# Retention attention and two feed-forward layers on one core: the causal upper quarter left out of the score products of eleven chunks, and the last output tile drained in two halves

## The chip, the cores and the metric

One core of a Trainium2 chip runs the kernel. The metric is the device time of one execution in microseconds, the median over runs of the same kernel. A profile of one execution goes with it: every instruction of every engine with its start and its length.

## What is computed

Four sequences of 576 tokens, eight heads of 64, pass through a causal attention without softmax whose scores are damped by a power of the distance, and then through two feed-forward layers. All of it is float32.

```python
scores = scale * np.matmul(q, k.transpose(0, 1, 3, 2))
Dmat = np.where(rel >= 0, gamma[:, None, None] ** rel[None, :, :], 0.0)   # rel = query - key position
ret = np.matmul(scores * Dmat, v)                     # x: (2304, 512) after the heads are joined
h = x @ w_in;  g = np.maximum(h, 0) + alpha * np.minimum(h, 0);  x = g @ w_out        # d_ff 2048
gate = 1 / (1 + np.exp(-(x @ w_gate)));  out = (gate * (x @ w_val)) @ w_out2          # d_ff 1536
```

## The kernel before, in words

The 2304 tokens are cut into five blocks (one of 256 tokens, four of 512) and, for the attention, into 20 chunks that lie inside one block and one sequence. Sixteen chunks have 128 tokens, four have 64. A chunk is processed as a step of a recurrence. The scores of the chunk's queries with the chunk's keys are formed (`att_scores`), multiplied by a 0/1 triangle on VectorE (the "mask"), and multiplied with the values (`att_values`). What earlier chunks of the sequence give is carried in a state `m_sb` (64x64 for each head): the queries are multiplied with it, and it is updated by the product of the chunk's keys and values. The damping sits in per-row factors that GpSimd multiplies into the queries (`att_q`, tile `qk`) and the values (`att_v`, tile `kv`) of the next chunk ahead of time.

Chunks 0 to 6 (blocks 0 and 1) run first, on banks of their own. Chunks 7 to 10 (block 2), 11 to 15 (block 3) and 16 to 19 (block 4) run in `att_stages`, in two stages each that are placed between the steps of the first feed-forward layer: a step `h` (12 products of 512 columns) and a step `y` (12 more). TensorE's order is the order of the code. For a chunk of 128 tokens in these blocks it reads: 8 score products (L571), a step of the layer, 8 products for the state's update (`m`, L597, absent for the last chunk of a sequence), 8 products of the queries with the old state (L600, absent for the first chunk of a sequence), 8 products of the scores with the values (L611), the next step. Chunk 10 begins a sequence; chunks 9 and 19 end one. Chunks 14 and 15 have 64 tokens.

All attention products are float32, and each is carried out as two passes, so that 8 products are 16 instructions in the trace. The products of the layers use split factors, with one instruction each (L700). A product with 64 rows or 64 columns of the array uses a part of it: the score products use 64 rows and 128 columns (written 64\*128 in the trace), the updates and the values 128\*64, the old state 64\*64. Two or four such products, on different parts, can be under way at once. The results of L600 and L611 add up in two banks, `o_0` and `o_1`, that held the scores `s_0` and `s_1`; so L600 waits until the masks of the chunk (L574, two on VectorE) have read them.

The order of the other engines' instructions is set by a scheduler at build time, with the times of a model. Each engine works off its instructions in that order, GpSimd too, and waits with all that is behind it when the first one waits. SyncE issues all transfers from one queue. At the end of the program, the last of 24 steps of the second layer's last block adds into two output tiles; ScalarE copies the first to SBUF, VectorE the second (`drain`, L733 to L740), and SyncE stores each.

Of the kernel before, what the change touches and what calls it, by code (L numbers as in the profile page):

```python
# [19 lines left out]
P = 128  # L20
# [66 lines left out]


CHUNKS = chunks()
LENGTHS = sorted({c[3] for c in CHUNKS})  # L90


O_M = NPAIR * P
O_GK = O_M + P
O_GP = O_GK + H
O_M2 = O_GP + len(LENGTHS) * NPAIR
O_GK2 = O_M2 + D
N_CST = O_GK2 + NPAIR


def constants():
    gamma = (1.0 - 2.0 ** (-5.0 - np.arange(H, dtype=np.float32))).astype(np.float64)
    i = np.arange(P)
    head = 2 * np.arange(NPAIR)[None, :] + (i // D)[:, None]
    out = np.zeros((P, N_CST), np.float32)
    out[:, :O_M] = (gamma[head][:, :, None] ** i / np.sqrt(D)).reshape(P, -1)
    out[:, O_M:O_GK] = i[None, :] >= i[:, None]
    out[:, O_GK:O_GP] = gamma ** -i[:, None].astype(np.float64)
    out[:, O_GP:O_M2] = (gamma[head][:, None, :] ** np.array(LENGTHS)[None, :, None]).reshape(P, -1)

    out[:, O_M2:O_GK2] = i[None, :D] >= i[:, None] % D
    out[:, O_GK2:] = gamma[head] ** -(i[:, None] % D).astype(np.float64)
    return out

# [2 lines left out]
def retention_two_ffn(ctx: ExitStack, tc: tile.TileContext, att, cst, alpha, w1, w2, out0, out1):  # L117
# [44 lines left out]
    mask = c_sb[:, O_M:O_GK]  # L162
    decay = c_sb[:, :O_M].rearrange("p (a i) -> p a i", a=NPAIR)


# [363 lines left out]
    def att_v(n):  # L529

        v = raw_a[n][1][:, 1]
        heads = v.shape[1]
        gk = O_GK if heads == H else O_GK2
# [10 lines left out]
    def att_scores(n, pool, tags):  # L544

        c = CHUNKS[n][3]
        qk = raw_a[n][0]
        if c < P:
            if len(tags) == 1:
                ps = pool.tile([P, 2, DM], F32, tag=tags, name=f"s{n}")[:, 0, :NPAIR * c]  # L550
                ps = ps.rearrange("p (a i) -> p a i", a=NPAIR)
            else:
                ps = pool.tile([P, NPAIR, c], F32, tag=tags[0], name=f"s{n}")
            for pr, e in HEADS:
                nc.tensor.matmul(ps[part(e), pr, :], qk[part(e), 1, pr, :], qk[part(e), 0, pr, :], start=True, stop=True)
            by = c_sb[:, O_M2:O_GK2].unsqueeze(1).to_broadcast([P, NPAIR, c])
            nc.vector.tensor_tensor(out=qk[:, 1], in0=ps, in1=by, op=ALU.mult)
            return qk[part(0), 1], qk[part(1), 1]
        if len(tags) == 1:
            ps = pool.tile([P, 2, DM], F32, tag=tags, name=f"s{n}")  # L560
            for pr, e in HEADS:
                nc.tensor.matmul(ps[:, e, pr * P:(pr + 1) * P], qk[part(e), 1, pr, :], qk[part(e), 0, pr, :], start=True, stop=True)
            s_sb = both_scores[n] = slot([P, 2, NPAIR, P], F32, f"sc{n}")
            nc.vector.tensor_tensor(
                out=s_sb.rearrange("p e a i -> p (e a) i"), in0=ps.rearrange("p e (a i) -> p (e a) i", a=NPAIR),
                in1=mask.unsqueeze(1).to_broadcast([P, H, c]), op=ALU.mult,
            )
            return s_sb[:, 0], s_sb[:, 1]
        ps = [pool.tile([P, NPAIR, P], F32, tag=tags[e], name=f"s{n}_{e}") for e in range(2)]
        for pr, e in HEADS:  # L570
            nc.tensor.matmul(ps[e][:, pr, :], qk[part(e), 1, pr, :], qk[part(e), 0, pr, :], start=True, stop=True)  # L571
        s_sb = qk[:, 1], small.tile([P, NPAIR, P], F32, tag="s", bufs=3, name=f"sc{n}")
        for e in (1, 0):
            nc.vector.tensor_tensor(  # L574
                out=s_sb[e], in0=ps[e], in1=mask.unsqueeze(1).to_broadcast([P, NPAIR, c]), op=ALU.mult,
            )
        return s_sb

    def att_values(n, s_sb, pool, tags):
# [13 lines left out]
        rows = lambda t, pr, e: kv[part(e), t, pr] if c < P else kv[:, t, 2 * pr + e]  # L593
        if not last:
# [3 lines left out]
        if pos:  # L598
            for pr, e in HEADS:
                nc.tensor.matmul(  # L600
                    out(pr, e), m_sb[part(e), pr, :], qk[part(e), 0, pr, :], start=pr < 2, stop=False,
                )
# [7 lines left out]
        for pr, e in HEADS:  # L610
            nc.tensor.matmul(  # L611
                out(pr, e), rows(1, pr, e), s_sb[e][:, pr, :], start=pos == 0 and pr < 2, stop=pr >= 2,
            )
# [563 lines left out]
    def plain_y(ps, g, f, first, last):  # L1177
        w = plain_outer[f]
        for e, t in enumerate(ps):

            r = tuple(w[:, :, i] for i in range(2))
            products(t.rearrange("p (c j) -> p c j", c=2), [(cols(g, e), r)], first, last)
            if last:
                drain(e, f"ost0_{e}", t, out0[e * P:(e + 1) * P, :])

    def plain_z(f, ws):
        nb = BLOCKS[0]
# [309 lines left out]
```

## Time and profile before

| | |
|---|---|
| median of 3 runs | 863.33 us (863.12 to 864.38) |
| the profiled execution's own time | 862.71 us |
| its span in the profile | 860.9 us |
| TensorE | 844.4 us busy, 98% |
| VectorE | 547.9 us, 64% |
| ScalarE | 419.7 us, 49% |
| GpSimd | 97.3 us, 11% |
| granted TensorE clock | 1.0 throughout |

A line of the timeline has the start in us, the length in us, the engine, the source line, the operation, the tiles (output<-inputs, without their numbers), the part of the array (rows\*columns) and the operand sizes, the count of instructions that are merged in it, and in brackets the idle time before it with what ended that. Matmul instructions overlap, so the time that a group of products costs is read from its start to the start of the next group, not from the length. In a line that ends in us, times, longest, the three figures are total waiting, count and the longest wait. PE is TensorE, DVE is VectorE, ACT is ScalarE, POOL is GpSimd, SP is SyncE.

### The profile page before, as it was taken

Reading aid. Unit: us, or ns where it says so; the run is one execution under the profiler, and the core shown is the slowest. Engines: PE = TensorE matmul, PEld = TensorE weight load, DVE = VectorE, ACT = ScalarE, POOL = GpSimd, SP = SyncE. Lnnn points to the kernel's source line nnn. Section 1 sums busy time; section 2 is a strip of 40 time slices with the busy share of each in tenths; the row PEclk is TensorE's granted clock in tenths of the full one; section 3 lists DMA queues with packets and bytes.
Section 4 is the critical chain, followed back from the end, with each engine's and each line's share of the span. In section 5 each row is a group of like instructions: output and inputs, shape, how many; then the busy total and the mean of one; then the engine's idle time right before and its main releaser. Section 6 shows DMA issues by size and latency. Waiting matters only on the chain.

```text
span 860.9 us, 13167 instructions
## 1 busy us (share of the span) xinstructions
PE 844.4 (98%) x4898; PEld 704.9 (82%) x4898; DVE 547.9 (64%) x840; ACT 419.7 (49%) x724; POOL 97.3 (11%) x72
## 2 busy tenths in 40 slices
PE   6899999999999999999999999999999999999998
PEld 5798888777778887888888888888888888888897
DVE  4899863785786969997647675469813332695111
ACT  1777754453564769986336653345412222352111
POOL 5357623223100000000000000000000000000000
PEclk9999999999999999999999999999999999999999
DMA  9658999699977125899967999255896561569970
GB/s 341 228 186 274 348 402 365 221 358 407 417 263 280 49 91 194 294 364 346 409 222 274 411 417 407 103 196 192 294 394 228 187 199 69 172 223 371 366 285 26
DMA packets 81728, 234.04 MB, mean 272 GB/s; under 512 B 8576, under 2 KB 9600, under 8 KB 81664
## 3 DMA queue, kind: packets, MB, share of 16 engines
q1 hardware_dynamic: 81664, 233.20, 73.9%
q8 instruction: 39, 0.64, 0.3%
q14 instruction: 25, 0.20, 0.1%
HBM read 169.72 MB, written 63.44 MB: 271 GB/s over the span
## 4 chain that ended last, share of the span: by engine, by line
PE 78%; DVE 1%; DMA 1%; ACT 1%; issue 0%; SPq 0%; DVEq 0%; ACTq 0%
PE a L700 15%; PE yy L700 10%; PE oa L700 8%; PE y L700 6%; PE h L700 5%; PE a_h L700 5%; PE z L700 4%; PE c L700 4%; PE b L700 4%; PE e L700 4%; PE o L700 2%; PE oc L700 2%; PE ob L700 2%; PE oe L700 2%; PE b_h L700 1%; PE c_h L700 1%
## 5 line engine op out<-in xcount | busy, mean ns | idle before, releaser
L700 PE MATMUL h<-x,w 128*128 128x512 f32 (+1 forms) x432 | 84.1, 346 | 2.1 <-DVE t L720 1.3
L700 PEld LDWEIGHTS h<-x,w 128*128 128x128 f32 x432 | 67.5, 190 | 12.6 <-DVE t L720 1.9
L700 PE MATMUL y<-g,w 128*128 128x512 f32 x240 | 58.9, 394 | 0.0
L336 ACT ACTIVATE q<-r 128x512 fp32r<-128x512 f32 x72 | 45.2, 664 | 24.3 <-PE yy L700 9.1
L231 POOL TENSOR_SCALAR r<-r 128x512 int32<-128x512 uint32 x26 | 51.9, 1996 | 42.2 <-DMA r<-w 30.1
L337 DVE TENSOR_TENSOR q<-r,q 128x512 fp32r<-128x512 f32 x72 | 49.3, 709 | 9.7 <-ACT q L336 9.7
L716 ACT ACTIVATE t<-h 128x512 f32<-128x512 f32 (+1 forms) x48 | 25.0, 521 | 57.8 <-PE h L700 57.8
L700 PEld LDWEIGHTS y<-g,w 128*128 128x128 f32 x240 | 44.4, 188 | 10.2 <-issue 1.0
L1029 DVE TENSOR_TENSOR c<-a,es 128x512 f32<-128x512 f32 x24 | 16.7, 699 | 55.3 <-PE a L700 55.3
L229 ACT ACTIVATE r<-r 128x512 f32<-128x512 f32 x68 | 45.0, 669 | 8.2 <-DMA r<-w 6.3
L238 DVE CUSTOM_DVE_ANT_0 r<-r,top 128x1024 uint16<-128x1024 uint16 x52 | 35.6, 696 | 2.3 <-POOL r L231 0.5
L700 PEld LDWEIGHTS z<-x,zp 128*128 128x128 f32 x288 | 36.0, 191 | 0.9
L700 PE MATMUL z<-x,zp 128*128 128x256 f32 x288 | 36.3, 283 | 0.0
L700 PE MATMUL h<-x,v 128*128 128x512 f32 x144 | 35.4, 395 | 0.0
L700 PE MATMUL y<-g,v 128*128 128x512 f32 x144 | 35.2, 393 | 0.0
L700 PEld LDWEIGHTS y<-g,v 128*128 128x128 f32 x144 | 26.7, 188 | 6.1 <-issue 0.7
L700 PE MATMUL a<-xf_1h,tq 128*128 128x512 f32 x96 | 31.5, 389 | 0.0
L700 PE MATMUL e<-xf_5h,tq 128*128 128x512 f32 x96 | 31.5, 389 | 0.0
L700 PE MATMUL a<-xf_6h,tq 128*128 128x512 f32 x96 | 31.5, 389 | 0.0
L700 PE MATMUL b<-xf_2h,tq 128*128 128x512 f32 x96 | 31.5, 389 | 0.0
L700 PE MATMUL a<-xf_7h,tq 128*128 128x512 f32 x96 | 31.5, 389 | 0.0
L700 PE MATMUL c<-xf_3h,tq 128*128 128x512 f32 x96 | 31.5, 389 | 0.0
(468 smaller groups left out, 2130.9 us busy)
## 6 DMA issues: line engine op xcount, KB each, us to landing
tq<-td SPq DMA_DIRECT2D x84, 512.0 KB, 7.1
r<-w SPq DMA_DIRECT2D x68, 512.0 KB, 6.5
wo<-wod SPq DMA_DIRECT2D x42, 512.0 KB, 4.8
v<-w1d SPq DMA_DIRECT2D x40, 512.0 KB, 6.0
td<-q SPq DMA_DIRECT2D x36, 512.0 KB, 5.1
wod<-q SPq DMA_DIRECT2D x24, 512.0 KB, 8.7
zp<-td SPq DMA_DIRECT2D x48, 256.0 KB, 5.8
w1d<-w SPq DMA_DIRECT2D x23, 512.0 KB, 8.5
```

Of the source, the lines that this page charges most:

```text
L229: nc.scalar.activation(high.bitcast(F32), high.bitcast(F32), AF.Prelu, scale=2.0 ** -112, alpha=2.0 ** 32)
L231: nc.gpsimd.tensor_scalar(low.bitcast(I32), low, 2.0 ** -29, None, ALU.mult)
L238: nc.vector.tensor_tensor(out=out.bitcast(I32), in0=low.bitcast(I32), in1=top.bitcast(I32), op=ALU.add)
L336: nc.scalar.activation(part[0], src, AF.Copy)
L337: nc.vector.tensor_tensor(out=part[1], in0=src, in1=part[0].bitcast(F32), op=ALU.subtract)
L700: nc.tensor.matmul(ps, l, r, start=first and i == 0, stop=last and i == len(todo) - 1, skip_group_check=joins)
L716: nc.scalar.activation(t, ps, AF.Relu)
L1029: nc.vector.tensor_tensor(out=c[q], in0=a[q], in1=es[q], op=ALU.add)
```

## The change

It has two parts.

1. In the eleven chunks of 128 tokens of blocks 2 to 4 (7 to 13 and 16 to 19), keys of the second half of a chunk are no longer multiplied with queries of the first half, whose product the triangle sets to zero. The score products have a stationary operand of 64 keys: for each head one with the early keys and all 128 queries, one with the late keys and the 64 late queries. They use 64\*64 of the array. Head pairs with an odd number have their halves exchanged, so that the four parts of the array hold early and late keys of even and odd pairs. The scores take 384 columns of a bank in place of 512, and so do the masks. The values are multiplied in two groups: late queries with all 128 keys (L658, 128\*64, 64 columns), then early queries with 64 keys (L664, 64\*64, 64 columns). The rows of keys and values of odd pairs are exchanged on the host, with the constants to fit; the table of constants grows from 724 to 796 columns. The old state's products move ahead of the update's. Since the early products add with one half of the array's rows into columns in which the other half's rows added the old state, a fence is put between them: GpSimd clears a tile `tick` of one column after the last product with the old state, and the first early product waits for it. Chunk 10 has no old state and no fence, so there are ten.
2. The second of the last two output tiles is copied in two halves, the left by VectorE and stored by SyncE, the right by ScalarE and stored from ScalarE's own queue.

```diff
+def changed_over(n):
+    return CHUNKS[n][0] > 1 and CHUNKS[n][3] == P
 ...
-        ps = [pool.tile([P, NPAIR, P], F32, tag=tags[e], name=f"s{n}_{e}") for e in range(2)]
-        for pr, e in HEADS:
-            nc.tensor.matmul(ps[e][:, pr, :], qk[part(e), 1, pr, :], qk[part(e), 0, pr, :], start=True, stop=True)
-        s_sb = qk[:, 1], small.tile([P, NPAIR, P], F32, tag="s", bufs=3, name=f"sc{n}")
+        ps = [two(pool.tile([P, DM], F32, tag=tags[e], name=f"s{n}_{e}")) for e in range(2)]
+        for g in range(NPAIR // 2):
+            for late in range(2):
+                for pr, e in HEADS[4 * g:4 * g + 4]:
+                    odd = pr % 2
+                    to = ps[e][part(late ^ odd), g]
+                    queries = qk[part(e), 0, pr, :].rearrange("p (h i) -> p h i", h=2)
+                    nc.tensor.matmul(
+                        to[:, 1 + odd] if late else to[:, 0:2 + odd:1 + odd], qk[part(e), 1, pr, part(late)],
+                        queries[:, 1] if late else queries, start=True, stop=True,
+                    )
 ...
         for e in (1, 0):
-            nc.vector.tensor_tensor(
-                out=s_sb[e], in0=ps[e], in1=mask.unsqueeze(1).to_broadcast([P, NPAIR, c]), op=ALU.mult,
-            )
+            nc.vector.tensor_tensor(out=flat(s_sb[e]), in0=flat(ps[e]), in1=by, op=ALU.mult)
 ...
+        if pos and changed_over(n):
+            a = from_state()
+            fence = nc.gpsimd.memset(tick, 0.0)
+            tc.add_manual_dep(fence.ins, a.ins.name, sync, reason="banks shared by two rows of the array")
         if not last:
             m_ps = ps_h.tile([P, NPAIR, D], F32, tag="h", name=f"m{n}")
 ...
+            for pr, e in HEADS:
+                nc.tensor.matmul(
+                    out(pr, e)[:, D:], rows(1, pr, e), s_sb[e][:, pr // 2, 1 + pr % 2],
+                    start=pos == 0 and pr < 2, stop=False,
+                )
+            for pr, e in HEADS:
+                at = part(pr % 2)
+                a = nc.tensor.matmul(
+                    out(pr, e)[:, :D], kv[at, 1, 2 * pr + e], s_sb[e][at, pr // 2, 0], start=False, stop=pr >= 2,
+                )
+                if fence and pr == 0:
+                    tc.add_manual_dep(a.ins, fence.ins.name, sync, reason="banks shared by two rows of the array")
 ...
-            if last:
+            if last and e == 0:
                 drain(e, f"ost0_{e}", t, out0[e * P:(e + 1) * P, :])
+            elif last:
+                st = half_slot_of(f"ost0_{e}")
+                for c, q in enumerate((nc.sync, nc.scalar)):
+                    at = slice(c * 256, (c + 1) * 256)
+                    if c:
+                        nc.scalar.activation(st[:, at], t[:, at], AF.Copy)
+                    else:
+                        nc.vector.tensor_copy(st[:, at], t[:, at])
+                    q.dma_start(out=out0[e * P:(e + 1) * P, at], in_=st[:, at])
+                free(st)
```

On TensorE, after the step `h` that follows chunk 7's scores, there stood before (`m` the update, `o` with `m_sb` the old state, `o` with `kv` the values; "waits" names what the instruction waits for, Pool being GpSimd):

```order
L597 MATMUL m_1790<-kv_1700 64x64 [waits DMAHW6_49,DVE_49,Pool_49]
L597 MATMUL m_1790<-kv_1700 64x64 x7
L600 MATMUL o_0_1788<-qk_1698,m_sb 64x128 [waits DVE_49,PE_49]
L600 MATMUL o_0_1788<-qk_1698,m_sb 64x128
L600 MATMUL o_1_1789<-qk_1698,m_sb 64x128 [waits PE_49]
```

and now:

```order
L628 MATMUL o_0_1797<-qk_1699,m_sb 64x128 x2
L628 MATMUL o_1_1798<-qk_1699,m_sb 64x128 x2
L641 MATMUL m_1808<-kv_1701 64x64 [waits DMAHW6_49,Pool_49]
L641 MATMUL m_1808<-kv_1701 64x64 x7
L658 MATMUL o_0_1797<-qk_1699,kv_1701 64x64
L658 MATMUL o_0_1797<-sc_1768,kv_1701 64x64
L658 MATMUL o_1_1798<-qk_1699,kv_1701 64x64
```

The update, which stood between the step and the first instruction that waits for the masks, now comes after it.

On GpSimd, for the chunks 14 to 17 (the number behind `qk` and `kv` is the chunk's), there stood before:

```order
L527 TENSOR_TENSOR qk15_2378<-qk15_2378,c_sb_86 128x256
L535 TENSOR_TENSOR kv15_2437<-kv15_2437,c_sb_86 128x256
L535 TENSOR_TENSOR kv16_2544<-kv16_2544,c_sb_86 128x512
L527 TENSOR_TENSOR qk17_2582<-qk17_2582,c_sb_86 128x512
L527 TENSOR_TENSOR qk16_2506<-qk16_2506,c_sb_86 128x512
L535 TENSOR_TENSOR kv17_2625<-kv17_2625,c_sb_86 128x512
```

and now:

```order
L540 TENSOR_TENSOR qk15_2488<-qk15_2488,c_sb_86 128x256
L548 TENSOR_TENSOR kv15_2556<-kv15_2556,c_sb_86 128x256
L636 MEMSET tick_194 128x1
L548 TENSOR_TENSOR kv16_2663<-kv16_2663,c_sb_86 128x512
L540 TENSOR_TENSOR qk17_2701<-qk17_2701,c_sb_86 128x512
L540 TENSOR_TENSOR qk16_2625<-qk16_2625,c_sb_86 128x512
L636 MEMSET tick_194 128x1
L548 TENSOR_TENSOR kv17_2744<-kv17_2744,c_sb_86 128x512
```

The two fences here are those of chunks 12 and 13: the first stands behind `kv15`, the second behind `qk17` and `qk16`. The fences of chunks 7, 8, 9 and 11 stand behind `qk9`, `qk10`, `kv11` and `kv13`, those of chunks 16 to 19 behind the last multiplication.

On VectorE the two masks of a chunk change places (the one that writes into `qk` comes first now), and one of the two subtractions of L337 that followed the masks of chunk 9 stands ahead of them.

At the end of the program ScalarE has now:

```order
L1260 ACTIVATE sg0_11_8169<-z0_11_8143 128x256 [waits PE_49,Activation_49]
L219 ACTIVATE p0_10_8134<-z0_11_8156 128x256 [waits DVE_49]
L793 ACTIVATE ost0_0_8183<-o0_0_7641 128x512 [waits PE_49]
L1246 ACTIVATE ost0_0_8183<-o0_1_7642 128x256 [waits DVE_49]
L1249 DMA y0<-ost0_0_8183 128x256 [waits DMAHW0_49,Activation_49]
```

The first two rows belong to the last step of the second layer's gate. Of the three behind them only the L793 was there before (as L738). The copy of the right half waits for VectorE, whose last instruction is the copy of the left half (L1248, which waits for TensorE).

## Rows read from the trace of the kernel before

**Rows 1.** The page: busy time by engine, and GB/s in 40 slices.
```profile
PE 844.4 (98%) x4898; PEld 704.9 (82%) x4898; DVE 547.9 (64%) x840; ACT 419.7 (49%) x724; POOL 97.3 (11%) x72
...
GB/s 341 228 186 274 348 402 365 221 358 407 417 263 280 49 91 194 294 364 346 409 222 274 411 417 407 103 196 192 294 394 228 187 199 69 172 223 371 366 285 26
```
**Rows 2.** Busy time in two stretches: length, then engines, clock, DMA share.
```profile
140.00:264.00 124.00, 123.53 (x1107) 95.95 (x1106) 88.83 (x162) 60.40 (x121) 25.57 (x22) 1.00 0.86 326
264.00:811.00 547.00, 546.90 (x2432) 453.01 (x2431) 345.99 (x479) 269.96 (x417) 0.00 (x0) 1.00 0.71 259
```
**Rows 3.** Timeline of TensorE, chunk 7.
```profile
140.85 1.16 PE L571 MATMUL s<-qk 64*128 64x128 f32 x16
141.95 3.02 PE L700 MATMUL h<-x,v 128*128 128x512 f32 x12
144.89 0.69 PE L597 MATMUL m<-kv 128*64 128x64 f32 x16
145.51 0.67 PE L600 MATMUL o<-qk,m_sb 64*64 64x128 f32 x16
146.11 0.32 PE L611 MATMUL o<-qk,kv 128*64 128x128 f32 x1
...
147.13 0.50 PE L700 MATMUL y<-g,w 128*128 128x512 f32 x1
```
**Rows 4.** Timeline of TensorE, old state and values of chunk 14 (64 tokens).
```profile
216.58 0.46 PE L600 MATMUL o<-qk,m_sb 64*64 64x64 f32 x16
216.86 0.41 PE L611 MATMUL o<-qk,kv 64*64 64x64 f32 x16
217.21 3.02 PE L700 MATMUL h<-x,w 128*128 128x512 f32 x12
```
**Rows 5.** Timeline of GpSimd, chunks 17 and 16.
```profile
204.74 1.28 POOL L527 TENSOR_TENSOR qk<-qk,c_sb 128x512 f32<-128x512 f32 x1 [1.46 <-DMA qk<-att]
206.56 1.28 POOL L527 TENSOR_TENSOR qk<-qk,c_sb 128x512 f32<-128x512 f32 x1 [0.55 <-ACT h L717]
```
**Rows 6.** Timeline of TensorE, chunk 13.
```profile
205.12 0.69 PE L597 MATMUL m<-kv 128*64 128x64 f32 x16
...
207.36 0.50 PE L700 MATMUL y<-g,w 128*128 128x512 f32 x1
```
**Rows 7.** SyncE from 200.5 to 201.2: its wait; what it issued (count, KB, us to landing).
```profile
SPq L506 <- DMA x2d<-yst: 0.6, 1, 0.6
...
qk<-att SPq DMA_DIRECT2D x1, 512.0 KB, 5.4
```
**Rows 8.** All transfers of tile qk.
```profile
DMA to landing us min/median/max: 3.5/6.7/9.6
```
**Rows 9.** Groups of GpSimd by line: count, busy us, mean ns.
```profile
L1485 POOL MEMSET const-float32-0.0<- 128x1 f32 x1 | 0.1, 100 | 0.2 <-issue 0.2
```
**Rows 10.** Masks of 512 columns (L574): ns, minimum, median, maximum.
```profile
L574 DVE TENSOR_TENSOR qk<-s,c_sb x11: 675/681/682, 142.7 to 260.9; 128x512 f32<-128x512 f32 x11
```
**Rows 11.** Masks of 256 columns (L557), of the 64-token chunks.
```profile
L557 DVE TENSOR_TENSOR qk<-s,c_sb x4: 411/420/426, 22.9 to 220.9; 128x256 f32<-128x256 f32 x4
```
**Rows 12.** Waits of TensorE for VectorE's masks, whole run.
```profile
PE o L600 <- DVE qk L574: 0.3, 1, 0.3
```
**Rows 13.** Timeline of all engines, chunks 9 (first row) and 18.
```profile
163.50 0.68 DVE L337 TENSOR_TENSOR q<-r,q 128x512 fp32r<-128x512 f32 x1
...
252.51 0.68 DVE L574 TENSOR_TENSOR qk<-s,c_sb 128x512 f32<-128x512 f32 x1
...
253.34 0.41 PE L600 MATMUL o<-qk,m_sb 64*64 64x128 f32 x5
```
**Rows 14.** Timeline of all engines, end of the program.
```profile
855.15 0.39 ACT L206 ACTIVATE p<-z 128x256 fp32r<-128x256 f32 x1 [1.51 <-DVE z L1195]
...
857.38 0.69 DVE L736 COPY ost<-o 128x512 f32<-128x512 f32 x1 [1.38 <-PE o L700]
```
**Rows 15.** Transfers issued after 850 us: count, KB, us to landing.
```profile
y<-ost SPq DMA_DIRECT2D x2, 256.0 KB, 2.0
```

More of the change, by code (lines that the diff above doesn't have):

```diff
@@ L106, in constants @@
     out[:, :O_M] = (gamma[head][:, :, None] ** i / np.sqrt(D)).reshape(P, -1)
[L107 to L111, printed above, removed]
+    half, at = i // D, i % D
+    causal = at[None, :D] >= at[:, None]
+    second = [np.where(half[:, None] == e, True, causal) for e in range(2)]
+    out[:, O_M:O_GK] = np.concatenate([causal & (half == 0)[:, None], causal, *second], axis=1)
+    by_head = out[:, O_GK:O_GK1] = gamma ** -i[:, None].astype(np.float64)
+    out[:, O_GK1:O_GP] = np.where(np.arange(H) // 2 % 2, np.roll(by_head, D, axis=0), by_head)
+    out[:, O_GP:O_GK2] = (gamma[head][:, None, :] ** np.array(LENGTHS)[None, :, None]).reshape(P, -1)
     out[:, O_GK2:] = gamma[head] ** -(i[:, None] % D).astype(np.float64)
@@ L160, in retention_two_ffn @@
     x2d = [dp.tile([P, KC, nb], F32, tag=f"x2d{j}", name=f"x2d{j}") for j, nb in enumerate(BLOCKS)]
-    mask = c_sb[:, O_M:O_GK]
+    masks = c_sb[:, O_M:O_GK].rearrange("p (h i) -> p h i", h=4)
+    tick = const.tile([P, 1], F32, tag="tick", name="tick")
     decay = c_sb[:, :O_M].rearrange("p (a i) -> p a i", a=NPAIR)
@@ L532, in att_v @@
         heads = v.shape[1]
-        gk = O_GK if heads == H else O_GK2
+        gk = (O_GK1 if changed_over(n) else O_GK) if heads == H else O_GK2
         by = c_sb[:, gk:gk + heads].unsqueeze(2).to_broadcast([P, heads, D])
@@ L555, in att_scores @@
                 nc.tensor.matmul(ps[part(e), pr, :], qk[part(e), 1, pr, :], qk[part(e), 0, pr, :], start=True, stop=True)
[L556 removed]
+            by = masks[:, 1].unsqueeze(1).to_broadcast([P, NPAIR, c])
             nc.vector.tensor_tensor(out=qk[:, 1], in0=ps, in1=by, op=ALU.mult)
@@ L593, in att_values, with from_state @@
         rows = lambda t, pr, e: kv[part(e), t, pr] if c < P else kv[:, t, 2 * pr + e]
+        fence = None
+        sync = mybir.DependencyInfo(mybir.DependencyClass.Sync, mybir.DependencyReason.DATA)
+        def from_state():
+            for pr, e in HEADS:
+                a = nc.tensor.matmul(
+                    out(pr, e), m_sb[part(e), pr, :], qk[part(e), 0, pr, :], start=pr < 2, stop=False,
+                )
+            return a
+        if pos and changed_over(n):
+            a = from_state()
+            fence = nc.gpsimd.memset(tick, 0.0)
+            tc.add_manual_dep(fence.ins, a.ins.name, sync, reason="banks shared by two rows of the array")
         if not last:
@@ L597, in att_values @@
                 nc.tensor.matmul(m_ps[part(e), pr, :], rows(0, pr, e), rows(1, pr, e), start=True, stop=True)
[L598 to L602, printed above, removed]
+        if pos and not fence:
+            from_state()
         if not last:
@@ L609, in att_values @@
             nc.vector.tensor_tensor(out=m_sb, in0=m_sb if pos else m_ps, in1=by, op=ALU.mult)
[L610 to L613, printed above, removed]
+        if not changed_over(n):
+            for pr, e in HEADS:
+                nc.tensor.matmul(
+                    out(pr, e), rows(1, pr, e), s_sb[e][:, pr, :], start=pos == 0 and pr < 2, stop=pr >= 2,
+                )
+        else:
+            for pr, e in HEADS:
+                nc.tensor.matmul(
+                    out(pr, e)[:, D:], rows(1, pr, e), s_sb[e][:, pr // 2, 1 + pr % 2],
+                    start=pos == 0 and pr < 2, stop=False,
+                )
+            for pr, e in HEADS:
+                at = part(pr % 2)
+                a = nc.tensor.matmul(
+                    out(pr, e)[:, :D], kv[at, 1, 2 * pr + e], s_sb[e][at, pr // 2, 0], start=False, stop=pr >= 2,
+                )
+                if fence and pr == 0:
+                    tc.add_manual_dep(a.ins, fence.ins.name, sync, reason="banks shared by two rows of the array")
         x = x_t[j]
@@ L1451 @@
     parts = []
-    for _, b, pos, c, _ in CHUNKS:
+    for n, (_, b, pos, c, _) in enumerate(CHUNKS):
         def cols(t):
@@ L1459, in rows @@
                 return t.reshape(NPAIR, 2, c, D).transpose(1, 2, 0, 3).reshape(P, NPAIR * D)
-            return t.transpose(1, 0, 2).reshape(P, H * D)
+            t = t.transpose(1, 0, 2).reshape(P, NPAIR, 2 * D)
+            if changed_over(n):
+                t = np.stack([np.roll(t[:, i], D, axis=0) if i % 2 else t[:, i] for i in range(NPAIR)], axis=1)
+            return t.reshape(P, H * D)
         parts.append(np.stack([cols(q), cols(k)], axis=1).ravel())
```

21 lines of the change are left out of this document (15 added, 6 removed).

## Prediction

> **What bounds the kernel now.** I first read the busy shares by engine: TensorE is busy 844.4 us of a span of 860.9, GpSimd only 97.3 [rows 1]. Then the two stretches that hold the changed chunks and all that follows them: TensorE is busy 123.53 us of 124.00 and 546.90 of 547.00, at a granted clock of 1.00, the full 2.4 GHz [rows 2]. So nothing else limits these stretches, and a microsecond taken from TensorE's attention work there reaches the end, as long as no new wait eats it. Next comes the timeline of TensorE for one chunk, where each group costs the time from its start to the next group's start [rows 3, 4]. Last come the queues that the new waits depend on: GpSimd around the fence of chunk 13, the transfer that it waits for there, and VectorE's masks [rows 5 to 8, 10 to 13].
>
> The profiled execution took 862.71 us, 0.62 below the median of 863.33. I make the sum as a difference and add it to the median.
>
> **Prices of products.** In chunk 7 the scores take 141.95 − 140.85 = 1.10 us, the update .62, the old state .60, the values (146.11 to 147.13) 1.02 [rows 3]. I call a "round" the passes that run side by side. The old state is 4 rounds of 128 columns and the values are 8, each with one change of the array's division: 4r + c = .60 and 8r + c = 1.02 give r = .105, c = .18. The scores are 8 rounds too, so their change costs .26. For 64 columns, state and values of chunk 14 are 8 rounds and a change in 217.21 − 216.58 = .63 [rows 4], so a round is .056; the update, 8 such rounds and a change in .62, says the same [rows 3].
>
> **Scores, eleven chunks.** Four rounds of 128 columns, four of 64 and one change: .42 + .22 + .18 = .82, or .90 with the dearer change, against 1.10. Gain .28 (bound .20) each, 3.1 in all.
>
> **Values, eleven chunks.** Late queries: 8 rounds of 64, .45, without a change where the update (also 128\*64) stands before them. Early queries: 4 rounds of 64 and a change, .40. Together .85 against 1.02, a gain of .17. In chunks 9 and 19 no update stands before them, and a change of .18 takes the gain away. Nine chunks give 1.5. With the scores 4.6 us; the lower bound, .20 for the scores and nothing for the values, is 2.2.
>
> A rule speaks against this. The row says that a round of 64 columns costs .056 and one of 128 .105 [rows 3, 4]. The Trainium skill, page "TensorEngine Tiling (Array Packing)", section "Performance Considerations" (Instruction Overhead), warns that each product has a fixed cost of about 60 cycles and that one should not take the tiling from a dimension that is already small. If that ruled here, shorter products would save nothing; the rows above put the step at a half, and go against it at 64 columns. It is the third rival below.
>
> **Masks.** The update stood between the step and L600, and covered the masks by .62 us [rows 3]. It moves behind L600. The scores end .28 earlier as well. The masks shrink from 512 columns (.68) to 384, between .68 and the .42 of 256 columns [rows 10, 11]; I take the middle, .55, so two masks end .26 sooner. In chunk 18 the second mask ends at 252.51 + .68 = 253.19 and L600 starts at 253.34 [rows 13]: no slack. There L600 now waits between .62 + .28 − .26 = .64, if VectorE is not moved by TensorE's lead, and .36, if the masks follow the scores by .28. Chunk 12 stands alike. In chunk 9, the only place where the masks held TensorE up before (.3) [rows 12], there is no update to move, but a subtraction of .68 [rows 13] now stands ahead of the masks: .28 + .68 − .26 = .70 at most. Chunk 19 has a little slack, 0 to .2. I take 1.2 for chunks 9 and 12, and .55 (bounds 0 and .8) for 18 and 19. The other chunks had slack of more than this, since TensorE did not wait at them.
>
> **The fence.** The memset itself is small: one of 128x1 took .10 us [rows 9]. What counts is GpSimd's order. For chunks 16 to 19 nothing stands before it. For chunk 13 the two multiplications for chunks 17 and 16 do: they ran at 204.74 and 206.56, the second to 207.84 [rows 5]. The second waited for its operand, a transfer issued near 200.9 that took 5.4 us [rows 7], to about 206.3. GpSimd started .25 later; I use this .25 for the step from GpSimd to TensorE too. Chunk 13's attention starts at 205.12 and ended at 207.36 [rows 6]. Without a fence its early products would be due at 205.12 + .60 + .62 + .45 = 206.79, less TensorE's lead. With it: landing L, + .25, + 1.28, + .10, + .25, and the early products of .40 behind: the next step starts at L + 2.28. With L as before, 208.58: **1.22 later than before, and all that was gained earlier is gone.** Who waits: the early products, and TensorE with all that is queued behind them; on GpSimd only the multiplication for chunk 17's values stands behind, with time to spare.
>
> L moves, though. SyncE's issue waited for the store of an earlier result of TensorE [rows 7], so it follows a part of TensorE's lead. The lead at chunk 11 is 5 × .28 + 4 × .17 − .65 (half of the 1.2, rounded up for chunk 9) = 1.4. If L follows entirely, 204.9, the step starts .18 sooner than before; if not at all, 1.22 later. The way from issue to landing is shared with other traffic (3.5 to 9.6 us for this tile, median 6.7) [rows 8], and 5.4 is on the short side. I take the half, L = 205.6 and a start .52 later than before.
>
> **After chunk 13.** Chunks 16 to 19: 4 × .28 + 3 × .17 = 1.63, less .55 for the masks: 1.1.
>
> **Start and end.** The larger table is 128 × 72 × 4 bytes = 37 KB; at the 341 GB/s of the first slice [rows 1] .1 at most, I take .05. At the end VectorE's copy, .69 from 857.38 [rows 14], shrinks to .42 (256 columns, [rows 11]), but ScalarE's half waits for VectorE and takes the .39 of a 256-column operation [rows 14]. The second store is issued near 857.38 + .42 + .39 = 858.19 plus a wait, against 858.07: .1 to .3 later, with half of the 256 KB whose landing took 2.0 us [rows 15]. Between −.15 and +.3; I take +.1.
>
> **Priced at nothing:** the new order of transfers on SyncE and of copies on ScalarE, while TensorE stays the busy engine of these stretches [rows 2]. If such a cover is gone, it is the second rival.
>
> **Sum.** +.52 − 1.1 + .05 + .1 = −.43: a median of 862.9. Its own range: L following entirely, masks free, −.18 − 1.63 − .15 = −1.96, so 861.4; L unmoved, low bounds for the gains (4 × .20 less .8 = 0), 1.22 + .1 + .3 = +1.62, so 865.0.
>
> **Rivals.**
> *1. The fence of chunk 13 is not in the way.* Then 4.6 less 1.2 and .55 for masks, plus .15: −2.7, 860.7. It needs GpSimd to be done with both multiplications by about 205.2 (206.79 less a lead of 1.3 and the .25), so a landing 2.7 us sooner than before, near the shortest way on record [rows 8], and the first multiplication sooner as well. For it: both move with the lead in part. Against it: the rows as they stand. Chance .15.
> *2. Slower: the transfer for chunk 16's multiplication lands later.* From there each microsecond of L is one of the end: the end moves by L − 206.03. It is slower by 1.7 from L = 207.8 on, a way of 7.6 us in place of 5.4. With 8.5 us, between median and maximum [rows 8], L = 208.7: +2.7, 866.0. For it: the reordered queue and the spread; against it: all the traffic moves together. Chance .10.
> *3. The short products don't pay.* If a round of 64 columns in the new divisions costs .105 (or the four parts don't overlap), the scores take .84 + .18 = 1.02, the values .84 and .42 + .18 = .60, 1.44 in all. Nine chunks lose .42 − .08 = .34, chunks 9 and 19, with the extra change of .18, .52: +4.1, with no stall at the fence, as TensorE comes later. 867.4. Against it: [rows 4]. Chance .05. This is also the case in which the change does not do what it says.
>
> **Chances.** Forecast .70, rivals .15, .10, .05. About 0.2%, 1.7 us, is what a measurement of this kernel can tell from no change. Of the forecast .03 falls below 861.6 and .02 above 865.1. So faster .18, same .65, slower .17. The range reaches to the first rival, 860.5, and to 865.0; it leaves out rivals 2 and 3 and the tails, nearly .2.
>
> **What would show it.** Scores of .82 and values of .85 on TensorE's timeline show the prices right; 1.0 and 1.4 show the third rival. A gap of 1 to 3 us ahead of the early products of chunk 13, ended by GpSimd, right behind its multiplication for chunk 16, shows the fence; no gap there, the first rival. Gaps of .3 to .7 ahead of L600's successor in chunks 9, 12 and 18, ended by VectorE, show the masks. The prediction is wrong if the lead survives chunk 13, or if a fence of chunks 7 to 11 holds TensorE up for longer than the lead gained until then.

## The result, and the profile of the changed kernel

The changed kernel takes 873.81 us (872.73 to 874.14, 4 runs) against 863.23 (862.78 to 864.38) of the kernel before: a ratio of 1.0119, 95% interval 1.0104 to 1.0134. It is 10.6 us slower. Forecast were 862.9 us and "about the same"; 866.0 and 867.4 were the slow rivals. The profiled execution took 873.51 us, its span is 871.7.

On the page TensorE is busier than before by 10 us, though it has less to multiply; compare [rows 1], whose first line answers to this one:

```profile
PE 854.1 (98%) x5250; PEld 705.6 (81%) x5250; DVE 546.6 (63%) x840; ACT 421.3 (48%) x725; POOL 97.7 (11%) x82
```

The two stretches of [rows 2] show two different losses. In the attention TensorE now has idle time (120.30 of 124). Behind it TensorE is busy without a gap, as before, but 2419 products stand in the 547 us where 2432 stood:

```profile
140.00:264.00 124.00, 120.30 (x1408) 92.92 (x1407) 85.94 (x159) 59.64 (x119) 26.07 (x31) 0.99 0.87 321
264.00:811.00 547.00, 547.00 (x2419) 445.63 (x2418) 346.41 (x480) 270.01 (x416) 0.10 (x1) 1.00 0.70 253
```

The second stretch is not the same work throughout in both, since the changed kernel runs some us later. A stretch in the middle of the plain products is cleaner: from 400 to 800 us, first the kernel before, then the changed one.

```profile
400.00:800.00 400.00, 400.00 (x1767) 331.20 (x1766) 228.46 (x297) 162.43 (x234) 0.00 (x0) 1.00 0.73 269
```
```profile
400.00:800.00 400.00, 400.00 (x1740) 326.17 (x1739) 230.87 (x301) 165.24 (x237) 0.00 (x0) 1.00 0.72 261
```

TensorE is busy all the time at the full clock (1.00) in both, and yet 27 products fewer have begun: on the mean they take 1.6% longer. Nothing in the change touches these products. By groups, in the changed kernel (last figure: mean ns of one), some are slow and some are not:

```profile
L755 PE MATMUL a<-xf_7h,tq 128*128 128x512 f32 x96 | 32.0, 394 | 0.0
L755 PE MATMUL b<-xf_2h,tq 128*128 128x512 f32 x96 | 31.5, 389 | 0.0
```

In the kernel before both have 389. A uniform cause, such as the clock, would slow both groups; this one depends on the tiles. Followed from step to step, the changed kernel is 3.3 us behind after chunk 19 (near 264 us) and 10.9 at the end: 7.6 us are lost in this second stretch, the rest before it.

Chunk 7 on TensorE answers to [rows 3] (L595 scores, L628 old state, L641 update, L658 late queries, L664 early queries):

```profile
141.54 0.90 PE L595 MATMUL s<-qk 64*64 64x128 f32 x32
142.37 3.06 PE L755 MATMUL h<-x,v 128*128 128x512 f32 x12
145.36 0.67 PE L628 MATMUL o<-qk,m_sb 64*64 64x128 f32 x16
145.96 0.69 PE L641 MATMUL m<-kv 128*64 128x64 f32 x16
146.47 0.22 PE L658 MATMUL o<-qk,kv 128*64 128x64 f32 x1
...
147.04 0.27 PE L664 MATMUL o<-qk,kv 64*64 64x64 f32 x1
```

From start to start the scores take .83, the old state .60, the update .51, the late queries .57, the early ones .39. Chunk 13, GpSimd and then TensorE, answers to [rows 5, 6]:

```profile
206.42 2.66 POOL L540 TENSOR_TENSOR qk<-qk,c_sb 128x512 f32<-128x512 f32 x2 [1.33 <-PE o L628]
209.02 0.10 POOL L636 MEMSET tick<- 128x1 f32 x1
```
```profile
206.70 0.22 PE L658 MATMUL o<-qk,kv 128*64 128x64 f32 x1
...
209.17 0.32 PE L664 MATMUL o<-qk,kv 64*64 64x64 f32 x1 [1.84 <-POOL tick L636]
...
209.79 4.35 PE L755 MATMUL y<-g,w 128*128 128x512 f32 x12
```

The early products wait 1.84 us for the fence (the memset of `tick`), which GpSimd clears behind both multiplications. The next step begins at 209.79, where it began at 207.36 before. And it takes 4.2 us in place of some 2.9. The window behind the wait shows why: the granted clock is .50, the 1.2 GHz level.

```profile
209.70:212.30 2.60, 2.60 (x14) 2.03 (x7) 1.47 (x3) 0.66 (x2) 0.00 (x0) 0.50 0.94 293
```

All waits of TensorE in this stretch, and the end of the program ([rows 14]):

```profile
PE o L664 <- POOL tick L636: 2.7, 2, 1.8
PE o L628 <- DVE qk L605: 0.8, 1, 0.8
```
```profile
868.23 0.42 DVE L1248 COPY ost<-o 128x256 f32<-128x256 f32 x1 [1.43 <-PE o L755]
868.68 0.34 SPq L1249 DMA_DIRECT2D y<-ost  x1
868.69 0.38 ACT L1246 ACTIVATE ost<-o 128x256 f32<-128x256 f32 x1 [0.56 <-DVE ost L1248]
869.10 0.38 ACTq L1249 DMA_DIRECT2D y<-ost  x1
```

ScalarE's half waits for VectorE's, as its order says. From VectorE's copy to the end of the span 3.5 us pass, as before (857.38 to 860.9): the halves bring and cost nothing.

### The profile page after: what moved, and what is told of

Its sections match the earlier page's. It is cut to its first block, busy times and chain, and to the rows that moved or that the text cites. A ratio compares the mean times of both kernels' runs of the same rounds, so it can differ in the third digit from the quotient of the medians.

```text
span 871.7 us, 13869 instructions
## 1 busy us (share of the span) xinstructions
PE 854.1 (98%) x5250; PEld 705.6 (81%) x5250; DVE 546.6 (63%) x840; ACT 421.3 (48%) x725; POOL 97.7 (11%) x82
## 4 chain that ended last, share of the span: by engine, by line
PE 75%; DVE 1%; ACT 0%; POOL 0%; issue 0%; POOLq 0%; DVEq 0%
PE a L755 15%; PE yy L755 10%; PE oa L755 8%; PE a_h L755 5%; PE y L755 5%; PE z L755 4%; PE e L755 4%; PE c L755 4%; PE b L755 4%; PE h L755 4%; PE o L755 2%; PE oe L755 2%; PE ob L755 2%; PE oc L755 2%; PE c_h L755 1%; PE b_h L755 1%
## 5 line engine op out<-in xcount | busy, mean ns | idle before, releaser
L755 PE MATMUL a<-xf_4h,tq 128*128 128x512 f32 x96 | 31.8, 392 | 0.0
L755 PEld LDWEIGHTS h<-x,v 128*128 128x128 f32 x144 | 26.5, 188 | 6.2
```

Of the source, the lines that this page charges most:

```text
L755: nc.tensor.matmul(ps, l, r, start=first and i == 0, stop=last and i == len(todo) - 1, skip_group_check=joins)
```

## Experiments

### Where the tiles stand in SBUF

The tile `tick` is 4 bytes a partition; in SBUF it takes 32. It is allocated ahead of nearly all tiles of the lower part, so these move by 32 bytes. The tiles of the upper part (allocated from the other end) stay. Some products have one operand in each part. Theory A says that the difference of the two operands' addresses costs; theory B looks for the cause in the attention.

`b_32` and `b_64`: the kernel before, with nothing added but a tile.

```diff
+    wedge = const.tile([P, 1], F32, tag="wedge", name="wedge"); nc.gpsimd.memset(wedge, 0.0)     # b_64: [P, 16]
```

> The kernel before with one more tile of 128x1 in SBUF (cleared once at the start), whose 32 bytes move the tiles behind it, in the lower part of SBUF, by 32 bytes against those in the upper part. Nothing else differs. Theory A (where the two operands of a product differ by 32 in their address modulo 64, the product of 512 columns takes some 233 ns in place of 227): the mean of these products rises to about 230 from 264 us on, and the kernel takes 870.5 to 872.5 us. Theory B (what slows the late part of the changed kernel comes from its attention products, its code or its clock, not from addresses): 863.2.

> The same with a tile of 64 bytes, so that addresses modulo 64 stay as they were. Theory A: 863.2 (+-0.5). Theory B: 863.2. Theory C (any move off a coarser boundary, 128 or 256 bytes, costs): 866 to 872.

`a_64` and `a_both32`: the changed kernel.

```diff
+    tick = const.tile([P, 16], F32, tag="tick", name="tick")[:, :1]      # a_64
+    pad_sb = pad.tile([P, 192], F32, tag="pad", name="pad_sb")           # a_both32, in place of 184
```

> The changed kernel with the fence's tile at 64 bytes in place of 32; the instructions are the same. Theory A: the 7.5 us that the trace shows lost after 264 us go, with about 1 before: 865.3 (864.5 to 866.5), products of 512 columns at 227 ns. What is left over the kernel before is the stall at the fence of chunk 13 with its slow clock behind it. Theory B: 873.8. Theory C: 868 to 874.

> The changed kernel with the pad at the upper end of SBUF 32 bytes longer, so that the upper tiles move by 32 bytes too: all tiles stand at 32 modulo 64, none at 0. Theory A in the form 'the two operands must differ': 866 to 867, nearly as a_64, since products with both at 32 took 227.5 ns in the changed kernel's trace. Theory A in the form 'any address off 64 costs': 874 or more. Theory B: 873.8.

Measured: `b_32` 871.6 us, ratio 1.0100 (1.0085 to 1.0115), so 8.2 us for 32 bytes, in an otherwise untouched kernel: theory B falls. But `b_64` takes 869.2 (1.0051 to 1.0088), and `a_64` 871.3, `a_both32` 871.7: agreement modulo 64 is not enough, and theory A missed in all three. Theory C, a coarser boundary, has the first two. (In `a_both32` the lower tiles stand 32 up and the upper ones 32 down, a difference of 64.) Larger wedges, and a tile that moves nothing, tell the grain:

```diff
+    wedge = const.tile([P, 32], ...)        # b_128; b_256: [P, 64]
+    tick = pad_sb[:, :1]                    # a_pad, the changed kernel
+    pad_sb = pad.tile([P, 240], ...)        # b_all32, beside the wedge of b_32
```

> The kernel before with the tile of b_32 and b_64 at 128 bytes. If the two operands of products must agree modulo 128: 863.4, products of 512 columns at 226.7 ns. If they must agree modulo 256 or more: 866 to 870.

> The same at 256 bytes. If agreement modulo 128 or 256 is enough: 863.4. If 512 or more is wanted: 866 to 870.

> The kernel before with the 32-byte tile of b_32 and the upper end's pad 224 bytes longer, so that all tiles, lower and upper, stand at 32 modulo 256. If only the difference of a product's two addresses counts: 863.4, with products of 512 columns at 226.7 ns. If the address itself counts: 868 to 872.

> The changed kernel with the fence's tile in the pad at the upper end of SBUF (tick is the pad's first column), so that every other tile stands where it stood in the kernel before, and the instructions are the same. Theory A (addresses cost the changed kernel some 8 us; the attention part itself costs what the stall at the fence of chunk 13 leaves): products of 512 columns back at 226.7 ns, 865.6 (863.0 to 867), that is the time before plus the 2.2 us between the changed kernel (873.8) and b_32 (871.6). Theory B (the slow late part does not come from addresses): 871 to 874.

| kernel | lower against upper tiles | products begun from 400 to 800 us | time, us | ratio to the kernel before |
|---|---|---|---|---|
| before | as built | 1767 | 863.2 | |
| b_32 | +32 bytes | 1739 | 871.6 | 1.0085 to 1.0115 |
| b_64 | +64 | 1745 | 869.2 | 1.0051 to 1.0088 |
| b_128 | +128 | 1743 | 870.6 | 1.0073 to 1.0102 |
| b_256 | +256 | 1767 | 863.5 | .9991 to 1.0013 |
| b_all32 | all at +32 modulo 256 | 1766 | 863.7 | .9993 to 1.0013 |
| after | +32 | 1740 | 873.8 | 1.0104 to 1.0134 |
| a_64 | +64 | 1745 | 871.3 | 1.0073 to 1.0123 |
| a_both32 | +32 against -32, 64 apart | 1744 | 871.7 | 1.0082 to 1.0122 |
| a_pad | as built | 1767 | 865.8 | 1.0015 to 1.0036 |

Of the offsets tried, the products are at their old pace where lower and upper tiles agree modulo 256 bytes, and only there (in the kernel before the build puts nearly all tiles at multiples of 256). `b_all32` says that it is the difference and not the address: with all tiles at 32 modulo 256, nothing is lost. The two groups shown above fit: `xf_2h` and its `tq` both lie in the lower part, `xf_7h` and its `tq` mostly (72 of 96 products) in different parts.

The trace and the addresses that the build gives the tiles allow the same test product by product. In the changed kernel, among the 1510 products of 512 columns from 486 us on, there are 535 that stream an operand of one part while their own weights and those of the next product stand in the other. They take 233.1 ns from start to start, and the same products take 226.8 in the kernel before. The 919 with all three in one part take 228.3 (226.9 before). In `a_pad` the two groups are back at 226.8 and 226.9.

With the tile in the pad the changed kernel is 8.0 us faster; that is the larger part of its loss. Why the chip does this no run shows. The Trainium skill says on the page "TensorE: Matmul & The Clock Gate" (Part 2, What happens when you issue a matmul) that loading the next weights takes no SBUF read bandwidth from the running product, since the two have ports of their own; but 31 products whose own two operands stand in one part, and only the next weights in the other, took 235.6 ns to the next start in place of 226.4, so the place of the next weights matters here, and the measurement decides. Whether the running product or the loading is held up, the trace does not tell.

### The fence and the transfers behind it

`a_pad` is still 2.6 us slower than the kernel before. Its fence of chunk 13:

```profile
206.38 2.82 POOL L540 TENSOR_TENSOR qk<-qk,c_sb 128x512 f32<-128x512 f32 x2 [1.48 <-DMA qk<-att]
209.14 0.10 POOL L636 MEMSET pad_sb<- 128x1 f32 x1
```
```profile
209.29 0.27 PE L664 MATMUL o<-qk,kv 64*64 64x64 f32 x1 [2.30 <-POOL pad_sb L636]
```

The fence is 2.0 us later than the prediction has it (205.6 + .25 + 1.28 = 207.13). Both multiplications waited for transfers. The one for chunk 16 (L in the prediction) was issued at 202.70 and took 4.8 us to land, at 207.5; before, it was issued at 200.88 and landed at 206.3. The issue in `a_pad`, and what SyncE waited for from 199 to 203 us, first before, then in `a_pad`:

```profile
202.70 0.33 SPq L519 DMA_DIRECT2D qk<-att  x1
```
```profile
SPq L506 <- DMA x2d<-yst: 2.2, 2, 1.6
```
```profile
SPq L519 <- DMA x2d<-yst: 3.6, 2, 2.8
```

The experiments that follow move the fence. `a_dve` moves all ten fences to VectorE, `a_mix` those of chunks 12 and 13 alone, `a_best` has in addition the update ahead of the old state in chunks 11, 12 and 18; all three have the tile in the pad. `b_fence` is the other side: the kernel before with this one fence (the scheduler also moves the transfer and the multiplication for chunk 19's `qk` by one place).

```diff
-            fence = nc.gpsimd.memset(tick, 0.0)
+            fence = nc.vector.memset(tick, 0.0)                                          # a_dve
+            fence = (nc.vector if n in (12, 13) else nc.gpsimd).memset(tick, 0.0)        # a_mix
+        if not last and n in (11, 12, 18): update()       # a_best: ahead of from_state()
```
```diff
+        if n == 13:                                        # b_fence
+            fence = nc.gpsimd.memset(pad_sb[:, :1], 0.0)   # behind the last product with the old state
```

> The kernel before with the fence alone, in chunk 13: GpSimd clears the pad's first column behind the last product with the old state, at the same place of its order as in the changed kernel (behind the multiplications for chunks 17 and 16), and the first product with the values waits for it. No product is changed. If the fence's place on GpSimd makes the loss: a gap of about 1.9 us ahead of the values of chunk 13 (GpSimd done at 207.94, the values due at 206.34), and slow products behind it for another 1.3: 866.4 (865 to 867.5). If the wait comes from what the changed products do to the transfers: under .5 of gap, 863.3.

Measured: 864.9 us, ratio 1.0027 (1.0015 to 1.0038), from the fence alone. In its trace GpSimd clears the tile at 206.99, and the values start at 207.15:

```profile
207.15 0.32 PE L616 MATMUL o<-qk,kv 128*64 128x128 f32 x1 [1.29 <-POOL pad_sb L606]
```

So a wait is made by the fence's place on GpSimd alone, 1.3 us in this execution. It is less than the 1.9 us expected, and the median lies just below the range of 865 to 867.5; in `a_pad`, where the transfers land later, the wait is 2.30. No slow products follow it here (granted clock 1.00 from 208.2 to 210.8); with 1.84 and 2.30 us they did.

> As a_pad, with the fence cleared by VectorE in place of GpSimd; there it stands right behind the masks of its chunk in all but one case. Theory A: no stall ahead of the early products in chunks 12 and 13 and no slow clock behind it; what stays are the shorter products less the waits for masks: 861.4 (860.5 to 862.5). Theory D (the stall is not GpSimd's order but any fence's round trip): as a_pad.

> As a_pad, with only the fences of chunks 12 and 13 on VectorE, the other eight on GpSimd. If what a_pad (865.8) loses is the stall at these two fences (.5 and 2.4 us in its trace) and the slow clock behind the second (some 1.4): 861.6 (861.0 to 862.5). If the lead that is kept only meets the next wait (masks behind VectorE's work on weights that transfers pace, as in chunk 19 of a_dve): 863 to 865.5, with the wait for masks in chunks 18 and 19 to be seen.

> As a_mix, and in chunks 11, 12 and 18 the update stands ahead of the old state again, as in the kernel before, to cover the masks. Each such chunk pays one more change of the array's division (.15 us), and saves the wait for masks, .45 in chunks 11 and 18 of a_pad. 861.2 (860.5 to 862.5) if nothing else takes the place; 863 to 865 if the lead meets the transfers.

Measured: `a_dve` 865.5 us (861.6 to 870.6), `a_mix` 866.8 (861.6 to 872.4), `a_best` 868.0 (865.3 to 870.4). All three missed; `a_dve` has the time of its theory D, but not by its mechanism. The stall at chunk 13 is gone in their traces, and what comes in its place varies from execution to execution, by up to 11 us. In `a_best` it was the GpSimd fence of chunk 11, 3.4 us. For the others more traces were taken:

> a_mix once more, for a second trace: its executions lie between 861.6 and 872.4, and the first trace is of one at 861.9. If what varies is waits of TensorE in the attention of blocks 2 to 4, and the slow clock behind them: an execution at 866 or more has two or more waits of over 1 us between 140 and 270 us, each with some six to nine products at .43 us behind it, and nothing different outside. If it is the pace of the products after 270 us: the mean of the 512-column products there is above 227 ns.

> A third trace of a_mix, with the same two answers expected as of the second: waits of over 1 us between 140 and 270 us with slow products behind them in an execution at 866 or more, or a slower pace of the products after 270 us.

> a_dve once more, for a second trace: executions between 861.6 and 870.6, the first trace of one at 863.0. Expected as for a_mix2: slow executions have waits over 1 us for masks or for transfers' work on VectorE or GpSimd, each followed by slow products.

| trace | its own time, us | wait for chunk 19's masks, us | moved by the transfers from 200 to 245 us, GB/s |
|---|---|---|---|
| a_dve2 | 861.8 | .2 | 406 |
| a_mix | 861.9 | 1.6 | 401 |
| a_dve | 863.0 | 1.5 | 400 |
| a_mix2 | 866.6 | 3.9 | 390 |
| a_mix3 | 867.7 | 5.2 | 380 |

The two slow executions have one long wait, in place of the "two or more" that were expected; among the three fast ones the wait does not order the times. VectorE and TensorE in `a_mix3`:

```profile
260.13 0.69 DVE L379 TENSOR_TENSOR s<-b 128x512 f32<-128x512 f32 x1 [6.72 <-DMA b<-w1f]
...
263.61 1.02 DVE L379 TENSOR_TENSOR wi<-b,wi 128x512 fp32r<-128x512 f32 x2
264.54 0.55 DVE L605 TENSOR_TENSOR qk<-s,c_sb 128x384 f32<-128x384 f32 x1
265.01 0.55 DVE L605 TENSOR_TENSOR sc<-s,c_sb 128x384 f32<-128x384 f32 x1
```
```profile
265.15 1.17 PE L628 MATMUL o<-qk,m_sb 64*64 64x128 f32 x12 [5.25 <-DVE qk L605]
```
```profile
265.15:268.30 3.15, 3.15 (x48) 2.46 (x48) 2.49 (x5) 2.04 (x4) 0.10 (x1) 0.50 0.74 294
```

VectorE idles 6.72 us for a transfer of weights (`b`, read from `w1f`), and five subtractions on `b` stand ahead of the masks in its order. Behind the wait TensorE works at .50 of its clock for 3 us more. The transfers themselves are the limit. From 200 to 245 us their share is 1.01, in the kernel before as in `a_mix3` (second to last figure):

```profile
200.00:245.00 45.00, 45.00 (x416) 34.95 (x416) 28.39 (x51) 20.68 (x42) 9.57 (x8) 1.00 1.01 403
```
```profile
200.00:245.00 45.00, 44.69 (x522) 35.13 (x521) 31.33 (x54) 21.88 (x44) 9.96 (x10) 1.00 1.01 380
```

And the waits of SyncE's queue from 238 to 253 us change their kind. Before, it waited for the engines; in `a_mix3` it waits for landings:

```profile
SPq L350 <- DVE q L337: 7.1, 3, 6.1
SPq L294 <- PE y L700: 1.8, 1, 1.8
```
```profile
SPq L307 <- DMA td<-q: 11.7, 3, 8.1
```

So the kernel before ran with both limits about equal in these 45 us, and a TensorE that is faster there outruns the transfers. How fast they are differs, and in the five traces of the table the wait grows as they get slower. That is an order in five traces, and no run changes the transfers alone to show it.

### The masks ahead of what waits for transfers

If that is the whole of it, the lead can be kept by letting nothing that a transfer paces stand ahead of the masks. `a_late` is `a_mix` with the five subtractions on `b` behind chunk 19's masks; VectorE's order is the only one that differs. `b_late` has the same order with the products of the kernel before. `a_late9` has in addition the subtraction of .68 us behind the masks of chunk 9 that stands ahead of them in the changed kernel (one store in SyncE's order moves with it).

```diff
         def sub(o, a, b):
             i = nc.vector.tensor_tensor(out=o, in0=a, in1=b, op=ALU.subtract)
+            if t == 1:
+                tc.add_manual_dep(i.ins, last_mask[0].ins.name, sync, reason="masks first")
```

> As a_mix, with one change on VectorE: the five subtractions of the weights' sums that a transfer paces (on b, read from w1f) and that stood ahead of chunk 19's masks stand behind them. If the wait for these masks (0 to 5.2 us in a_mix's three traces, with slow products behind it) is what spreads a_mix over 861.6 to 872.4 and eats its lead: a narrow spread, within 2 us, and 860.6 (859.8 to 861.8), with TensorE some 2.9 us ahead of the kernel before at 246 us and still ahead at the end. If the lead only meets the transfers at another place: 863 or more, with a new wait behind chunk 19.

> As a_late, and the subtraction of .68 us that stands ahead of chunk 9's masks on VectorE stands behind them. The wait there (.8 us in a_mix, and 1.2 of lead lost at that chunk) shrinks by .5 to .7: 860.0 (859.2 to 861.5) if that lead is kept. If the transfers between 200 and 245 us take any lead: as a_late.

> The kernel before with the same five subtractions behind chunk 19's masks. TensorE did not wait for these masks there, so the order alone should bring nothing: 863.2 (+-0.4). If the order alone brings the gain of a_late: 860 to 861.

Measured: `a_late` 861.6 us, ratio .9985 (.9974 to .9997), 859.7 to 864.7, a wider spread than expected; `a_late9` 861.0, .9974 (.9965 to .9983), 859.0 to 861.6; `b_late` 863.3, 1.0003 (.9995 to 1.0012). The order alone does nothing, the shorter products without it lost time (`a_mix`, 866.8), both together gain 2.2 us over the kernel before and 12.8 over the changed one. In `a_late9` the masks of chunk 19 run as soon as the scores are there, and `b` comes behind:

```profile
257.23 0.56 DVE L621 TENSOR_TENSOR qk<-s,c_sb 128x384 f32<-128x384 f32 x1 [0.54 <-PE s L611]
257.70 0.55 DVE L621 TENSOR_TENSOR sc<-s,c_sb 128x384 f32<-128x384 f32 x1
258.17 0.68 DVE L387 TENSOR_TENSOR s<-b 128x512 f32<-128x512 f32 x1
```

All that TensorE waits for between 140 and 270 us in it, where `a_pad` waits 2.7 us at the fence alone:

```profile
PE o L644 <- DVE qk L621: 0.4, 2, 0.2
```

## Why the prediction was wrong, point by point

**What bounds the kernel.** Here lies the main failure. The prediction says that nothing but TensorE limits the two stretches, and treats the pace of the products from 264 us on as given. This is the step that failed. The new tile was priced by its memset alone (.10 us); its place in SBUF had no term. It cost 8.0 us of the 10.6 (`after` against `a_pad`; 8.2 in `b_32`). The diff shows the new tile in a pool that was allocated ahead of others, and that was the place to ask which tiles move.

The second half of the same step failed too. [rows 2] has the DMA share of .86 for 140 to 264 us, a mean that was passed over; in 200 to 245 us it is 1.01. TensorE busy all the time and transfers busy all the time are not exclusive, and a gain on one then ends at the other.

**Prices of products: right.** Scores .83 (forecast .82), but for chunk 9, where they took 1.15 in the changed kernel; why stays open. Update, late and early queries 1.47 with the old state's .60 unchanged; before, update and values took 1.64, so .17 is gained, as forecast. Inside that sum the change of division sits elsewhere: the update takes .51 where .62 was assumed, the late queries .57 where .45 was. The Trainium skill's warning on tilings of an already small dimension ("TensorEngine Tiling (Array Packing)", Instruction Overhead), which was the third rival (scores of 1.02, late and early queries of 1.44), is not borne out at 64 columns: the scores took .83, the late and early queries .96.

**Masks: the right mechanism.** A mask of 384 columns took .55, as assumed. The wait at chunk 9 was .8 us (forecast .70 at most), .2 once the subtraction was moved. It cost more than its length: the second half of the old state's products then waits for the second mask, so the old state took 1.05 in place of .60, and from the start of the step to the values it took 4.94 us, 1.0 more than before. Chunk 12, which was to wait like chunk 18, did not wait. Chunk 11 in `a_pad` waited .5, where the prediction named no place. The bound of .8 for chunks 18 and 19 held in `a_pad`; it did not once the lead was kept, when chunk 19 waited up to 5.2.

**The fence: the right place and cause, the wrong size.** The next step began 2.43 us later than before (2.32 in `a_pad`), where .52 was forecast and 1.22 was the bound. The term that was mis-sized is L, the landing of chunk 16's transfer: 205.6 was forecast, 206.3 if it did not move at all, and it was 207.5. With that, the prediction's L + 2.28 gives 209.8, and 209.79 was measured. L was let follow half of TensorE's lead; the transfer was issued 1.8 us later than before instead, since SyncE waited 3.6 us for the store that the prediction names (199 to 203 us in `a_pad`; 2.2 before). The first of the two multiplications, for which the prediction has no term, started 1.6 us late as well (206.38 in place of 204.74), and would alone have kept the second to 207.65. The assumed lead of 1.4 was not there either: the step ahead of this fence began at 202.29 in `a_pad` and 202.17 before, as the waits at chunks 9 and 11 and the fence of chunk 12 had taken what was gained. This is the second rival's mechanism, a late transfer, which had a chance of .10. That its time of 866.0 is so near to `a_pad`'s 865.8 is luck: it has L at 208.7, after a slow landing; by its own sum the measured L gives 1.5 us, to 864.8, and the rest comes from the slow clock, which it lacks.

**The clock: no term at all.** The step behind the fence took 4.44 us in `a_pad` where it took 2.85 before, 1.6 more (seven products at .43 where .23 is usual). A stall was priced by its length alone.

**After chunk 13: .8 to .9 in place of 1.1.** In `a_pad` the lag fell from 3.92 us ahead of chunk 16 to 3.06 behind chunk 19; chunks 16 and 17 gave .43 each and chunk 19 .28, chunk 18 took .25 back.

**Start and end.** The tail is unchanged (forecast +.1). The first product of the layer starts between .3 earlier and 2.1 later than before in the traces of the kernels with the larger table, and 1.2 later in `b_32`, which has the old one. In the eight traces with the old table it starts between 29.21 and 30.75 us, in the twelve with the larger one between 28.96 and 31.35: the start varies by more than the table could cost, and what the table costs stays open.

Also open is what makes `a_late` spread over 5 us (in its one trace, of an execution at 863.6, the scores of chunk 7 begin 1.3 us later than before, chunk 11 waits .5 for its masks, and TensorE waits .5 for ScalarE at 269 us), and whether the waits in the executions of which no trace exists were at the same places.

## What to carry to other kernels

Ask of every new tile which others it moves: here 4 bytes ahead of the pools cost 8 us, nearly four times what the change won at its best (2.2), at places that the change does not touch, and it looked like a busy TensorE. Count the products in a window of fixed length to see such a loss. Where TensorE is busy without a gap, look at the DMA share of short windows before promising a gain: where it was 1.0 as well, shorter products paid here only once nothing that waits for a transfer stood ahead of what TensorE waits for, on VectorE and on GpSimd.

## What the runs showed of the hardware

- Products of 512 columns took 1.3 to 1.6% longer on the mean when tiles of the lower and the upper part of SBUF differed by 32, 64 or 128 bytes modulo 256, and no longer when they agreed (1739 to 1745 products in 400 us against 1766 to 1767). All tiles at 32 modulo 256 cost nothing. Busy shares, clock and waits show no trace of it.
- Behind waits of TensorE of 1.84, 2.30, 3.4, 3.9 and 5.2 us in the attention of blocks 2 to 4 the granted clock fell to half for a few us, which cost 1.2 to 1.6 us more; behind waits of 1.3 and 1.6 us it stayed at full. The length of the wait alone does not decide it. Near 25 us TensorE waits for `m_sb` in every kernel: 2.07 us in the kernel before and 3.1 in `b_64`, with the clock at 1.00 behind it, and 2.04 in the changed kernel, with .58. Wait and clock (third figure from the end), before and then changed:

```profile
26.54 0.46 PE L600 MATMUL o<-qk,m_sb 64*64 64x64 f32 x16 [2.07 <-DVE m_sb L609]
28.00:30.00 2.00, 2.00 (x36) 1.83 (x33) 2.00 (x7) 0.83 (x2) 0.65 (x1) 1.00 0.26 99
```
```profile
26.98 0.41 PE L628 MATMUL o<-qk,m_sb 64*64 64x64 f32 x13 [2.04 <-DVE m_sb L650]
28.00:30.00 2.00, 2.00 (x36) 1.93 (x33) 2.00 (x6) 1.26 (x3) 0.00 (x0) 0.58 0.46 170
```
